# Late rows gathered by two transfers, early tiles added singly, 8 KB store runs, and batch 0's q as f32 at the head of SyncE's queue

## The chip, the cores and the metric

The kernel runs on one core of one Trainium2 chip. The metric is device microseconds of that core: the median of several executions, all fast unless said otherwise (one execution of the kernel before, 435.10 us, was slow and is left out). Profiles are single executions, and their span is some 2 us shorter than the timed execution.

TensorE (PE) does the matrix products, VectorE (DVE) and ScalarE (ACT) the elementwise work. SyncE (SP) and GpSimd (POOL) mostly issue transfers. The profile counts 16 DMA engines, and all transfers are shown on them.

## The reference

Linear attention with an ELU feature map is followed by a spectral mix, for 8 batches, 8 heads, 576 positions and head size 64 (so D = 512):

```python
q_p, k_p = phi(q), phi(k)                       # phi(x) = where(x > 0, x, exp(x) - 1) + 1
kv  = einsum('bhsd,bhse->bhde', k_p, v);  z = sum(k_p, axis=2)
x   = (q_p @ kv) / (q_p . z)                    # reordered to (B, S, D)
X   = rfft(x, axis=1)[:, :64]                   # 64 modes
Y   = X @ (w_r + i w_i), one complex 512x512 matrix for each mode
u   = x + irfft(Y);  out = u + relu(u @ w_ch)   # f32, 9.44 MB
```

The weights w_r and w_i are 64 matrices each of 512x512 f32, 134 MB in all. Reading them is the bulk of the work.

## The kernel before

The kernel has three stages. First, attention and forward transform, while q, k, v and the first weights arrive. Then the 64 modes, one pair of weight matrices after another, cast from f32 to bf16 by the transfer. Last, a tail after the final weights: the last 8 modes' contribution is added to every output tile, and the tiles are stored. A tile is 128 rows of 512 f32, 2 KB to a partition.

The loads of the start; all three inputs are cast to f16 by transfers that GpSimd issues:

```python
nc.sync.dma_start(out=id16, in_=id16_dr.ap())         # at the head of SyncE's queue
nc.sync.dma_start(out=fwd_sb, in_=fwd_dr.ap())
...
def load(b):
    for nm, src in (("q", q), ("k", k), ("v", v)):
        t = sA.tile([128, NHP, NJ * Dh], F16, tag=f"{nm}16", bufs=2, ...)
        pin(nc.gpsimd.dma_start(out=t, in_=src[b] ...))
```

In the tail, the last modes' rows (`last`: 128 partitions of mode, real/imaginary, batch; a y half and a z half, 2 KB together) are moved to where the later products want them. For each batch that is partitions 48 to 63 and again 112 to 127 of the tile `YZ[b]`:

```python
for b in (2, 3, 0, 1, 4, 5, 6, 7):
    for h in range(1 if b < N_LEAD else 2):           # 14 transfers of 32 KB
        nc.gpsimd.dma_start(out=YZ[b][64 * h + 48 : 64 * h + 64, :, :], in_=last[b::B, :, :])
```

The tiles of batches 0 and 1 use `last` directly. From the fifth pair of tiles on, the product reads `YZ`. Each pair is finished by a product, one VectorE add of 1024 columns and one store:

```python
def finish(n):                                        # cut
    add_inverse(n, 0)                                 # TensorE, reads last or YZ
    on_bank(n, {0, 1}, nc.vector.tensor_tensor(out=x, in0=acc, in1=x, op=ALU.add))
    store(t0, 2)                                      # SyncE: 512 KB in runs of 4 KB
...
store(0, 1); relu(0, 1); rectified(1); channels(2)
add_inverse(0, 0, (1,)); ...add of tile 1...; store(1, 1)
channels(3); rectified(2); finish(1)
rectified(3); finish(2)
```

## Time and profile before

| | |
|---|---|
| time, median of 3 (429.36 us of 6, later) | 429.39 us (428.43 to 429.47) |
| DMA share of the chain that ended last | 73% |
| last product with the final weights starts | 394.31 us |
| first store issued | 398.08 us |
| last add on VectorE ends | 420.14 us |
| span | 427.4 us |

The profile's page of the kernel before. The two rows cover the span in 40 equal slices: the mean busy share of the DMA engines in tenths, and what they moved in GB/s. The last line gives the chain of waits by engine.

```profile
DMA  8999999999999999999999999999999999996698
GB/s 146 207 208 209 209 210 209 211 214 214 218 212 214 213 214 213 215 212 214 213 213 214 213 214 212 214 214 214 214 213 214 214 214 212 213 213 135 211 404 313
DMA 73%; PE 12%; DVE 6%; issue 5%; POOL 1%; ACT 1%; DVEq 0%; POOLq 0%
```

DMA is busy nearly throughout. The slices from 385 to 395 us (135 GB/s, the last weights and the start of the tail) and from 395 to 406 us (211 GB/s) are the slack ones; the second is well short of the roughly 400 GB/s that stores reach afterwards. (The row counts the casting loads by the bytes they write. The page has 82.26 MB in their queue and 163.93 MB read from memory, so they read twice as much.)

### The profile page before, as it was taken

To read this page: it belongs to the slowest core of one execution; us is meant where nothing else is said; L and a number is where in the kernel's file an instruction comes from. 1 tells how busy PE (TensorE), PEld (TensorE's weight loads), DVE (VectorE), ACT (ScalarE), POOL (GpSimd) and SP (SyncE) were. 2 spreads that over 40 slices of the span, in tenths; PEclk is the share of its full clock that TensorE was granted. 3 is DMA by queue.
4 is the path that set the end of the run, shared out by engine and by line. 5 is a ranking of instruction groups with operands and counts; after the bars stand their busy time and mean duration, and the time that the engine had idled before them with its cause. 6 is when DMAs were issued, how large, how long until landed. Compare 5 with 4: busy or idle time off the path is not lost.

```text
span 427.4 us, 6617 instructions
## 1 busy us (share of the span) xinstructions
PE 285.4 (67%) x2692; PEld 158.9 (37%) x2692; DVE 212.1 (50%) x432; ACT 153.7 (36%) x240; POOL 95.6 (22%) x173
## 2 busy tenths in 40 slices
PE   0357777788119765655333697777788788999991
PEld 0346655564003433333111333433333344374320
DVE  0699998956003755556200433443354344421893
ACT  3588666640102100000000244444353353431781
POOL 4233223212201322112112122122122122010600
PEclk9996666656557755555555569999898899799996
DMA  8999999999999999999999999999999999996698
GB/s 146 207 208 209 209 210 209 211 214 214 218 212 214 213 214 213 215 212 214 213 213 214 213 214 212 214 214 214 214 213 214 214 214 212 213 213 135 211 404 313
DMA packets 35854, 92.46 MB, mean 216 GB/s; under 512 B 3216, under 2 KB 16400, under 8 KB 35824
## 3 DMA queue, kind: packets, MB, share of 16 engines
q0 software_dynamic: 32256, 82.26, 99.0%
q1 hardware_dynamic: 3568, 9.78, 6.0%
q8 instruction: 21, 0.34, 0.3%
q14 instruction: 9, 0.07, 0.0%
HBM read 163.93 MB, written 9.44 MB: 406 GB/s over the span
## 4 chain that ended last, share of the span: by engine, by line
DMA 73%; PE 12%; DVE 6%; issue 5%; POOL 1%; ACT 1%; DVEq 0%; POOLq 0%
DMA wr<-in_moe_w_r_dram 48%; DMA wi<-in_moe_w_i_dram 13%; DMA pick_sb<-row_pick 4%; DMA q<-in_q_dram 4%; DMA k<-in_k_dram 4%; PE P L349 3%; PE acc L616 3%; DVE x L267 2%; PE acc L655 2%; PE z L579 1%; PE zb L606 1%; PE eps L557 1%; PE zb L605 1%; DVE qe L195 1%; ACT ke L182 1%
## 5 line engine op out<-in xcount | busy, mean ns | idle before, releaser
L349 PE MATMUL P<-wi,xt_c 128*32 128x512 bf16 x252 | 37.8, 536 | 39.7 <-DMA wi<-in_moe_w_i_dram 39.7
L360 ACT CAST ys<-P 128x512 f16<-128x512 f32 x31 | 18.2, 586 | 125.3 <-PE P L349 125.3
L110 POOL DMA_DIRECT2D wr<-in_moe_w_r_dram x64 | 34.0, 532 | 124.4 <-PE P L349 102.2
L110 POOL DMA_DIRECT2D wi<-in_moe_w_i_dram x65 | 34.5, 531 | 117.7 <-PE P L349 82.8
L358 DVE CAST ys<-P 128x512 f16<-128x512 f32 x32 | 22.1, 691 | 72.3 <-PE P L349 72.2
L349 PEld LDWEIGHTS <-xt_c 128*32 128x32 bf16 x504 | 28.9, 155 | 76.3 <-issue 65.2
L349 PE MATMUL P<-wr,xt_c 128*32 128x512 bf16 x252 | 37.5, 532 | 23.0 <-DMA wr<-in_moe_w_r_dram 20.8
L538 DVE TENSOR_TENSOR x_main<-ya,x_main 128x512 f32<-128x512 f32 x32 | 22.1, 691 | 39.7 <-PE ya L534 39.6
L557 PE MATMUL eps<-wch,xTw 128*128 128x512 f16 x144 | 41.3, 415 | 0.0
L146 PEld LDWEIGHTS <-qT 64*128 64x128 f16 (+1 forms) x640 | 23.3, 126 | 41.1 <-issue 20.7
L365 PE MATMUL yt<-pick_sb,ys 128*128 128x16 f16 x252 | 16.5, 175 | 25.5 <-DMA pick_sb<-row_pick 15.1
L540 ACT CAST x16w<-x_main 128x512 f16<-128x512 f32 x32 | 19.8, 618 | 34.7 <-DVE x_main L538 34.7
L565 ACT CAST E<-eps 128x512 f16<-128x512 f32 (+1 forms) x40 | 21.3, 543 | 26.6 <-PE eps L557 26.6
L146 PE MATMUL num<-kv,qT 64*128 64x65 f16 (+1 forms) x320 | 13.5, 223 | 22.5 <-ACT kv L242 18.7
L365 PEld LDWEIGHTS <-ys 128*128 128x128 f16 x252 | 12.2, 102 | 40.5 <-issue 17.8
L182 ACT ACTIVATE qe<-q 128x1152 f16<-128x1152 f16 x16 | 17.7, 1155 | 22.7 <-DMA q<-in_q_dram 22.7
L211 PE MATMUL qTp<-id,qe 128*128 128x128 f16 x144 | 16.8, 312 | 12.4 <-DVE qe L195 12.0
L267 DVE TENSOR_TENSOR x<-num,rd 128x512 f16<-128x512 f32 x32 | 22.1, 692 | 1.1
L146 PE MATMUL nw<-kv,qT 64*128 64x65 f16 (+1 forms) x320 | 19.6, 236 | 1.1 <-DVE x_tail L508 0.9
L211 PEld LDWEIGHTS <-qe 128*128 128x128 f16 x144 | 14.7, 147 | 13.2 <-DVE qe L195 12.0
L182 ACT ACTIVATE ke<-k 128x1152 f16<-128x1152 f16 x16 | 17.7, 1155 | 4.9 <-DMA k<-in_k_dram 4.9
L665 ACT ACTIVATE acc<-acc 128x512 f32<-128x512 f32 x34 | 18.1, 581 | 2.3 <-PE acc L616 1.7
(101 smaller groups left out, 451.8 us busy)
## 6 DMA issues: line engine op xcount, KB each, us to landing
wr<-in_moe_w_r_dram POOLq DMA_DIRECT2D x64, 512.0 KB, 18.8
wi<-in_moe_w_i_dram POOLq DMA_DIRECT2D x63, 512.0 KB, 18.9
out_dram<-x_main SPq DMA_DIRECT2D x14, 512.0 KB, 5.8
q<-in_q_dram POOLq DMA_DIRECT2D x8, 576.0 KB, 13.1
k<-in_k_dram POOLq DMA_DIRECT2D x8, 576.0 KB, 14.5
v<-in_v_dram POOLq DMA_DIRECT2D x8, 576.0 KB, 16.7
out_dram<-x_main SPq DMA_DIRECT2D x4, 256.0 KB, 3.6
out_dram<-x_tail SPq DMA_DIRECT2D x2, 512.0 KB, 5.3
```

Of the source, the lines that this page charges most:

```text
L110: tc.keep_in_program_order(nc.gpsimd.dma_start(out=w[:, dcs], in_=rows_of[:, dcs, :]))
L146: mm = nc.tensor.matmul(num[hpo][orow, c0 : c0 + 65], qT[rows, hpp, h2, cols], kv_sb[rows, hpp, h2, :])
L182: pin(nc.scalar.activation(out=ev[:, c], in_=heads(nm, b)[:, c], func=AF.Exp))
L211: nc.tensor.transpose(qT_ps[:, j].rearrange("p t r -> p (t r)"), phi["q", b][:, hpp, j].rearrange("p o d -> p (o d)"), id16,)
L267: nc.vector.tensor_tensor(out=dst.rearrange("p (o c d) -> p o c d", o=2, c=4), in0=nv[:, :, :, 0:64], in1=rden.unsqueeze(3).broadcast_to([ ...
L349: nc.tensor.matmul(P[dc * 32 : dc * 32 + 32, :], xt_cols(dc, t, kk), w[:, dc, :], start=(t == 1), stop=(t == 0), tile_position=(0, dc * 32),)
L358: fixed(nc.vector.tensor_copy(out=st, in_=P))
L365: nc.tensor.matmul(yt_ps[:, ec, kk % 8, :], st[:, ec * 128 : ec * 128 + 128], pick_sb)
L538: pin(nc.vector.tensor_tensor(out=x, in0=acc, in1=x, op=ALU.add))
L540: pin(nc.scalar.copy(out=x16w[t], in_=x))
L557: nc.tensor.matmul(e_ps, xT[:, c, :], wch16[:, c, :], start=(c == 0), stop=(c == NDC - 1))
L565: pin(nc.scalar.copy(out=dst, in_=e_ps[:, cols]))
```

## The change

The change has five parts. Batch 0's q is loaded without a cast (f32) from the head of SyncE's queue, so that bytes move before GpSimd's first cast load. The 14 small gathers become two, one on SyncE and one on GpSimd. Tiles 2 and 3 are added and stored singly, so that stores start sooner. Batches 4 to 6 are stored as four tiles at once, in runs of 8 KB. The transposed last rows are copied in halves by two engines. The diff, cut to its core:

```diff
-    nc.sync.dma_start(out=id16, in_=id16_dr.ap())
-    nc.sync.dma_start(out=fwd_sb, in_=fwd_dr.ap())
...
+            if (nm, b) == ("q", 0):
+                for c in range(2):
+                    t = sA.tile([128, 2, NJ * Dh], F32, tag="x16", bufs=2, name=f"q32_{c}")
+                    pin(nc.sync.dma_start(out=t, in_=rows_in[:, c::2, :]))
+                    raw[nm, b, c] = t
+                pin(nc.sync.dma_start(out=id16, in_=id16_dr.ap()))
+                pin(nc.sync.dma_start(out=fwd_sb, in_=fwd_dr.ap()))
+                continue
...
-    YZ = [sW.tile([128, 2, D], F16, tag="YZ", bufs=B, name=f"YZ{b}") for b in range(B)]
+    YZ_all = sW.tile([128, B, 2, D], F16, tag="YZ", bufs=1, name="YZ_all")
+    YZ = [YZ_all[:, b] for b in range(B)]
...
+    QUADS = (4, 5, 6)
...
+        if t0 < B * NJJ and t0 // NJJ in QUADS:
+            if t0 % NJJ:
+                store(t0 - 2, NJJ)
+            return
...
-    pin(nc.scalar.copy(out=last[:, 0, :], in_=y_ps.rearrange("p c r -> p (c r)")))
+    pin(nc.scalar.copy(out=last[:, 0, COLS[0]], in_=y_ps[0].rearrange("p c r -> p (c r)")))
+    pin(nc.vector.tensor_copy(out=last[:, 0, COLS[1]], in_=y_ps[1].rearrange("p c r -> p (c r)")))
...
-    for b in (2, 3, 0, 1, 4, 5, 6, 7):
-        for h in range(1 if b < N_LEAD else 2):
-            nc.gpsimd.dma_start(out=YZ[b][64 * h + 48 : 64 * h + 64, :, :], in_=last[b::B, :, :])
+    for h, eng in enumerate((nc.sync, nc.gpsimd)):
+        eng.dma_start(
+            out=YZ_all[64 * h + 48 : 64 * h + 64].rearrange("r b z d -> r b (z d)"),
+            in_=last.rearrange("p z d -> p (z d)"),
+        )
...
-    channels(3)
     rectified(2)
-    finish(1)
+    for i in range(2):
+        add_inverse(1, 0, (i,))
+        add_one(1, i)
+    channels(3)
     rectified(3)
```

## The prediction

> **What bounds it now.** The page's DMA row is at 9 tenths in nearly every slice, the software queue takes 99% of 16 engines' span, and the chain of waits is 73% DMA, nearly all weight loads. The other engines have slack until the last weights land (394.3 us, timeline). Then a 33 us tail writes 9.44 MB. There the packet records show about 403 GB/s from 406 us to 425.5 us, while the last add on VectorE ends at 420.1 us: the stores are DMA-bound too, with some 4 us of backlog at the end. Only from 399 to 406 us does DMA run short: 145 to 370 GB/s, a loss of about 1.9 us of full-rate transfer.
>
> **The change, piece by piece.**
>
> 1. *Batch 0's q as f32 on SyncE's queue.* Before, the first cast load issues at 1.26 us and moves bytes from about 3.5 us; the identity and DFT loads at SyncE's head issue at 0.74 us and move from 1.9 us, only 0.19 MB. After, 1.18 MB of q moves from about 2.0 us at some 390 GB/s (estimate), and one 2.85 us cast load leaves GpSimd's queue. About 1.5 us of empty DMA is filled; the 0.19 MB comes later, costing about 0.7 us (73 ns a packet of 1280 B, 17 ns one of 256 B, 16 engines). Net 0.6 to 0.8 us; it reaches the end, as the stream has no gap up to 390 us.
>
> 2. *Late rows by two transfers.* 14 issues of 0.48 us on GpSimd (397.2 to 403.9 us) become two, one on SyncE. TensorE does not wait for them now, so the gain is indirect: 0.5 MB moves before the first store, where DMA is empty (394.3 to 398.5 us), not between stores. The Trainium skill ("DMA: Bandwidth & Descriptors", "Issuing engines are not separate DMA queues") says all queues share the 16 engines; the trace agrees: the stores' rate falls to 235 GB/s where row packets interleave.
>
> 3. *First four tiles singly.* Tiles 2 and 3 are stored about 1.2 and 0.6 us sooner, filling the hole at 401 us. Two more stores of 2 KB runs cost 0.1 us (87 ns per 2 KB, 163 per 4 KB). Items 2 and 3 together: 1.2 to 1.8 us.
>
> 4. *8 KB runs, batches 4 to 6.* At best 3 to 4% on 3.1 MB (estimate), 0.25 us. Holding the first pair back 1.14 us should just be covered by the backlog.
>
> 5. *Transposed last rows copied by halves, copies moved.* The zl products keep TensorE busy until 396.0 us, so y0 starts no earlier: 0 to 0.1 us.
>
> **Sum.** 0.7 + 1.5 + 0.2 = 2.4 us, all on the DMA path. Predicted 427.0 us, 8 in 10 between 425.4 and 428.6. Faster by over 2%: 1%; within 2%: 98%; slower: 1%.
>
> **What would show it.** Right: last weights land 0.5 to 1 us earlier; the first transfer carries q at about 2 us; two row transfers land before about 400.5 us; the DMA rate stays above 350 GB/s from 400 us; the first store stays about 3.8 us after the last weights land; tail 1.5 to 2 us shorter; 8 KB packets take under 326 ns. Wrong: the weights end unmoved (item 1), a DMA hole at 409 to 412 us (item 4), TensorE waiting for YZ (item 2).
>
> **What would make it wrong.** A gather that writes 16 partitions at a low rate and blocks stores; SyncE issuing the gather so slowly that the first store slips; the slow DMA engine, which ends 4 us after the others, not profiting from item 1.

## More of the kernel before

The tail of the kernel before, in stretches of 2 us. Columns: the stretch, then busy us of PE, PEld, DVE, ACT and POOL with instruction counts, TensorE's granted clock, DMA share, GB/s. (The share adds up the times of all packets, so it can exceed 1 where packets of one engine overlap.)

```profile
396.00:398.00 2.00, 1.70 (x9) 0.71 (x8) 1.66 (x3) 0.80 (x3) 0.77 (x2) 1.00 0.00 0
398.00:400.00 2.00, 2.00 (x11) 0.99 (x10) 0.99 (x3) 1.82 (x4) 2.00 (x5) 1.00 0.56 189
400.00:402.00 2.00, 2.00 (x10) 0.75 (x9) 2.00 (x2) 1.75 (x5) 2.00 (x5) 1.00 0.69 238
402.00:404.00 2.00, 2.00 (x12) 0.41 (x10) 2.00 (x3) 1.72 (x5) 1.92 (x5) 1.00 0.96 341
404.00:406.00 2.00, 2.00 (x16) 0.68 (x14) 1.97 (x3) 1.73 (x4) 0.00 (x0) 1.00 0.96 341
406.00:408.00 2.00, 2.00 (x14) 0.60 (x14) 1.94 (x2) 1.71 (x4) 0.00 (x0) 1.00 1.03 412
```

Two different shortages stand here. Until 402 us the engines are partly idle (0.56, 0.69). From 402 to 406 us they are busy (0.96) and yet move only 341 GB/s.

The transfers issued from 396 to 405 us in the kernel before; the last figure is the median of us from issue to landing:

```profile
out_dram<-x_main SPq DMA_DIRECT2D x2, 256.0 KB, 2.6
YZ<-last POOLq DMA_DIRECT2D x14, 32.0 KB, 2.8
```

## The result, and the profile after

The changed kernel takes 429.2 us (428.75 to 430.86, 6 runs), the kernel before 429.36 us in the same rounds. The ratio is 1.0003, with a 95% interval of 0.9983 to 1.0023. Ratios here and below are the mean time of one kernel's fast runs over that of the other's of the same rounds, so they are not quite the ratio of the medians. Where a ratio is turned into microseconds, it is its distance from 1 times 429.4 us. A gain of 2.4 us was forecast and none came. A second job read the same (after_again, 1.0004).

The tail of the changed kernel, in the same stretches and columns:

```profile
396.00:398.00 2.00, 1.95 (x9) 0.99 (x9) 1.45 (x3) 1.27 (x3) 0.56 (x1) 1.00 0.31 61
398.00:400.00 2.00, 2.00 (x10) 0.95 (x9) 1.72 (x3) 1.87 (x5) 0.00 (x0) 1.00 1.16 172
400.00:402.00 2.00, 0.82 (x4) 0.22 (x2) 1.22 (x1) 0.89 (x2) 0.00 (x0) 1.00 0.92 153
402.00:404.00 2.00, 1.47 (x7) 0.49 (x8) 0.51 (x1) 0.75 (x2) 0.00 (x0) 1.00 1.06 393
404.00:406.00 2.00, 2.00 (x13) 0.56 (x10) 2.00 (x3) 1.72 (x4) 0.00 (x0) 1.00 0.89 362
406.00:408.00 2.00, 2.00 (x17) 0.58 (x15) 1.97 (x2) 1.61 (x4) 0.00 (x0) 1.00 1.00 401
```

From 398 to 402 us the DMA share is about 1, so the engines are fully occupied, and they move only 172 and 153 GB/s. From 400 us TensorE runs dry (0.82 us of 2), and from 402 us VectorE (0.51 us of 2). The waits of VectorE and TensorE from 396 us on in the changed kernel say for what; the figures are us in total, times, longest:

```profile
DVE x_main L708 <- PE acc L627: 2.6, 2, 2.2
PE acc L627 <- DMA YZ_all<-last: 1.7, 2, 1.0
```

The kernel before had no wait of TensorE on `YZ` in its tail, and VectorE's adds there waited 0.6 us at most:

```profile
DVE x_main L695 <- PE acc L616: 0.6, 1, 0.6
```

The transfers issued from 395 to 400 us in the changed kernel, with the us from issue to landing:

```profile
out_dram<-x_main SPq DMA_DIRECT2D x4, 256.0 KB, 5.2
YZ_all<-last SPq DMA_DIRECT2D x1, 256.0 KB, 5.1
YZ_all<-last POOLq DMA_DIRECT2D x1, 256.0 KB, 6.2
```

A store of one tile takes 5.2 us where it took 2.6. Tile 0's store is issued at 397.37 us, and the packet records show no packet of any store before 400.48 us. The gathers' packets run from 397.3 to 401.2 us: 524 KB in 3.8 us, 137 GB/s (128 to 145 GB/s in the four profiles that have two whole gathers). GpSimd's 4 KB packets take 599 ns at the median, and 16 engines at 4096 B in 599 ns are 109 GB/s. (That is this profile; in after_again, the same kernel, the median is 498 ns.)

The gain at the start is there. The kernel before, then the changed kernel, from 0 to 6 us, same columns:

```profile
0.00:2.00 2.00, 0.00 (x0) 0.00 (x0) 0.63 (x3) 1.27 (x1) 0.94 (x5) 1.00 0.07 16
2.00:4.00 2.00, 0.00 (x0) 0.00 (x0) 0.00 (x0) 0.22 (x2) 2.00 (x4) 1.00 0.72 121
4.00:6.00 2.00, 0.00 (x0) 0.00 (x0) 0.00 (x0) 0.00 (x0) 1.89 (x3) 1.00 1.16 172
```

```profile
0.00:2.00 2.00, 0.00 (x0) 0.00 (x0) 0.63 (x3) 1.27 (x1) 0.95 (x5) 1.00 0.15 13
2.00:4.00 2.00, 0.00 (x0) 0.00 (x0) 0.00 (x0) 0.22 (x2) 2.00 (x4) 1.00 0.85 275
4.00:6.00 2.00, 0.00 (x0) 0.00 (x0) 0.18 (x1) 1.16 (x1) 1.87 (x3) 1.00 1.08 354
```

The plain f32 load moves 275 GB/s where the old queue heads moved 121. (The f32 bytes count in full, the cast ones by half.) The first store is issued at 397.37 us instead of 398.08 us.

### The profile page after: what moved, and what is told of

Its sections match the earlier page's. It is cut to its first block, busy times and chain, and to the rows that moved or that the text cites. A ratio compares the mean times of both kernels' runs of the same rounds, so it can differ in the third digit from the quotient of the medians.

```text
span 427.8 us, 6610 instructions
## 1 busy us (share of the span) xinstructions
PE 281.6 (66%) x2692; PEld 158.3 (37%) x2692; DVE 214.5 (50%) x434; ACT 154.1 (36%) x241; POOL 88.1 (21%) x159
## 4 chain that ended last, share of the span: by engine, by line
DMA 67%; PE 15%; DVE 7%; issue 7%; ACT 1%; POOL 1%; DVEq 0%; POOLq 0%; ACTq 0%
DMA wi<-in_moe_w_i_dram 43%; DMA wr<-in_moe_w_r_dram 14%; DMA k<-in_k_dram 9%; PE P L359 3%; PE acc L627 2%; DVE x L277 2%; PE z L590 2%; PE acc L666 2%; DMA YZ_all<-last 1%; ACT ke L190 1%; PE zl L345 1%; PE yp L603 1%; PE zb L617 1%; PE zb L616 1%; PE eps L568 1%
## 5 line engine op out<-in xcount | busy, mean ns | idle before, releaser
L359 PE MATMUL P<-wi,xt_c 128*32 128x512 bf16 x252 | 36.2, 517 | 42.2 <-DMA wi<-in_moe_w_i_dram 42.1
L568 PE MATMUL eps<-wch,xTw 128*128 128x512 f16 x144 | 40.3, 407 | 0.0
L190 ACT ACTIVATE qe<-q 128x1152 f16<-128x1152 f16 (+1 forms) x16 | 17.8, 1156 | 18.0 <-DMA q<-in_q_dram 17.9
```

The lines of the kernel that those rows point to most:

```text
L190: pin(nc.scalar.activation(out=ev[:, c], in_=heads(nm, b, c), func=AF.Exp))
L359: nc.tensor.matmul(P[dc * 32 : dc * 32 + 32, :], xt_cols(dc, t, kk), w[:, dc, :], start=(t == 1), stop=(t == 0), tile_position=(0, dc * 32),)
L568: nc.tensor.matmul(e_ps, xT[:, c, :], wch16[:, c, :], start=(c == 0), stop=(c == NDC - 1))
```

## The experiments

**Theory 1 (ports).** A gather of 262 KB into 16 neighbouring partitions moves at about a quarter of the full rate, because those partitions share few SBUF ports. The Trainium skill ("SBUF — State Buffer", "Door 1: The DMA port swizzle") says that groups of four partitions share a port, that partitions 0 to 15 reach 4 of 16 ports and about 109 GB/s at best, 32 neighbours 8 ports, and all 128 all 16. By its table, partitions 48 to 63 lie on ports 8, 10, 12 and 14. If that holds here, the two gathers occupy all DMA engines for nearly 4 us, keep the first stores back and starve TensorE of `YZ`.

**Theory 2 (quads).** The loss comes from holding back half of batches 4 to 6, so that DMA runs short at 413 us. The changed kernel's DMA share from 412 to 416 us was 0.93 against 1.03 before. The kernel before, then the changed kernel, same columns:

```profile
412.00:416.00 4.00, 4.00 (x26) 1.15 (x26) 3.97 (x4) 3.51 (x7) 0.00 (x0) 1.00 1.03 406
412.00:416.00 4.00, 4.00 (x22) 0.89 (x22) 4.00 (x4) 3.63 (x8) 0.00 (x0) 1.00 0.93 370
```

**Theory 3 (SyncE's queue).** The gather stands ahead of the stores in SyncE's queue and keeps them back by its place, not by its rate.

**Theory 4.** The early load gains nothing at the end, because the slowest DMA engine does not profit.

### The gather undone, the gather alone

a_gather14 is the changed kernel with the old 14 gathers:

```diff
-    for h, eng in enumerate((nc.sync, nc.gpsimd)):
-        eng.dma_start(out=YZ_all[64 * h + 48 : 64 * h + 64].rearrange(...), in_=last.rearrange(...))
+    for b in (2, 3, 0, 1, 4, 5, 6, 7):
+        for h in range(1 if b < N_LEAD else 2):
+            nc.gpsimd.dma_start(out=YZ[b][64 * h + 48 : 64 * h + 64, :, :], in_=last[b::B, :, :])
```

> The changed kernel with the late rows gathered by the old 14 small transfers; all else kept. Ports theory (two gathers of 262 KB, each written into 16 neighbouring partitions, move at about 108 GB/s, hold every DMA engine from 397.6 to 401.4 us, keep the first stores back and starve TensorE, VectorE idle 2.2 us): the first stores move by 398.5 us, VectorE has no wait over 1 us in the tail, time 426 to 427.5 us. Quad theory (the loss comes from holding back half of batches 4 to 6): the hole at 413 us stays and the time stays at 428.5 us or more.

b_gather2 is the kernel before with the opposite edit alone.

> The kernel before with the two gathers alone. Ports theory: slower by 1.5 to 3 us (431 to 432.5 us), with TensorE waiting on YZ for 1 to 2 us and the stores of tiles 0 and 1 not moving before about 400.5 us. Quad theory: within 0.5 us of before.

a_gather14 read 428.19 us, ratio to before 0.9966 (0.9945 to 0.9988). b_gather2 read 430.73 us, ratio 1.0023 (1.0000 to 1.0047), about 1.0 us slower (1.25 by the medians; the interval just reaches none). Both moved in the direction of theory 1, both by less than it expected: a_gather14's median lies above the stated 426 to 427.5 us, and b_gather2's below the stated 431 to 432.5 us. In the traces, a_gather14's first store packet moves at 397.65 us, as expected; b_gather2's moves at 399.58 us, earlier than the expected 400.5.

The tail of a_gather14, same columns:

```profile
396.00:398.00 2.00, 2.00 (x11) 0.89 (x10) 1.48 (x3) 1.83 (x4) 2.00 (x5) 1.00 0.28 96
398.00:400.00 2.00, 2.00 (x11) 0.86 (x9) 1.66 (x3) 1.78 (x4) 2.00 (x5) 1.00 0.84 272
400.00:402.00 2.00, 2.00 (x12) 0.61 (x10) 1.90 (x3) 1.49 (x3) 2.00 (x6) 1.00 0.94 318
402.00:404.00 2.00, 2.00 (x16) 0.68 (x14) 2.00 (x3) 1.73 (x4) 0.46 (x1) 1.00 0.96 344
```

TensorE and VectorE no longer run dry. From 398 to 402 us the engines move 272 and 318 GB/s instead of 172 and 153, at shares of 0.84 and 0.94 instead of 1.16 and 0.92. VectorE waits 0.8 us for the add of tile 0, as in the changed kernel, and at most 0.4 us for any later add. The store of one tile lands in 2.9 us again:

```profile
out_dram<-x_main SPq DMA_DIRECT2D x4, 256.0 KB, 2.9
```

a_gather14 also makes `YZ` eight tiles again. That is not the cause: probe_end below keeps `YZ_all` as one tile beside the 14 gathers, and TensorE has no wait on it in its tail.

The kernel before with the two gathers shows the new waits, here of VectorE and of TensorE:

```profile
DVE x_main L696 <- PE acc L617: 3.9, 4, 2.5
PE acc L617 <- DMA YZ_all<-last: 1.7, 1, 1.7
```

VectorE waits 3.9 us and the time grows by only about 1.0 us. This is consistent with the backlog of stores at the end of the kernel before: VectorE's last add ends at 420.1 us, the span at 427.4 us. VectorE has slack to lose, and the time depends on what the DMA engines carry. (A lowered granted clock may be part of the 3.9 us: TensorE had 0.50 from 404 to 406 us in this profile.)

To read the cost on one chip, the changed kernel and a_gather14 were run once more together.

> The changed kernel once more, on one chip with the next two, so that the cost of the gathers is read from the same rounds. If the gathers cost what the traces suggest (first store to last packet 28.5 us against 26.9 us): 1.2 to 1.7 us slower than a_gather14_again and equal to before within 0.8 us.

> a_gather14 once more: 0.9945 to 0.9985 of before. If it is no faster than after_again here, the gather is not the cause and the earlier difference lay between the chips.

(The spans of 28.5 and 26.9 us in the first of these are not found again in the traces: from the issue of the first store to the end of the last packet they give 29.2 and 27.9 us.)

after_again read 429.52 us, ratio 1.0004 (0.9987 to 1.0021). a_gather14_again read 427.87 us, ratio 0.9961 (0.9949 to 0.9973). The two gathers cost 1.65 us by the medians and 1.84 us by the means, at or just above the upper end of the expected 1.2 to 1.7. The two large gathers also carry 65 KB more than the 14, which skip the second half for batches 0 and 1; how much of the cost that is was not tested. The cost is as much as all the other parts of the change gain together.

### Is it the place in the queue?

a_gather2_pool is the changed kernel with both gathers on GpSimd:

```diff
-    for h, eng in enumerate((nc.sync, nc.gpsimd)):
+    for h, eng in enumerate((nc.gpsimd, nc.gpsimd)):
```

> The changed kernel with both gathers issued by GpSimd, so that SyncE's queue holds stores alone. Ports theory: no better than the changed kernel, 429 to 430.5 us, with the same wait of TensorE for YZ. Rival, that the gather ahead of the stores on SyncE's queue keeps them back: 428 to 428.4 us, as a_gather14.

It read 430.98 us, ratio 1.0048 (1.0023 to 1.0073), slower than both expectations. Freeing SyncE's queue does not help, so theory 3 falls. The packet records show how: tile 0's store is issued at 399.02 us and its packets start at 400.41 us, sooner after the issue than in the changed kernel (1.4 against 3.1 us), but the first 128 store packets then take 3.1 us instead of 1.6. Held back or slowed, 262 KB are out 4.5 to 4.7 us after the issue, against 1.7 us in a_gather14. Why it is slower still than the changed kernel is not settled. Its profiled run also shows TensorE's granted clock at 0.72 from 396 to 400 us, where the changed kernel had 1.00, so its tail began late for a reason of its own.

### The disputed rate by itself

probe_end is a_gather14 (with `YZ_all` as one tile) and six transfers after the last store, each waiting for the one before, all with the same 128 source runs of 2 KB:

```diff
+    x_end = x_of(pairs[-1][1])
+    nc.vector.memset(x_end, 0.0)                      # waits for the last store
+    for z in range(2):
+        nc.vector.tensor_copy(out=last[:, z, :], in_=x_end)
+    for eng in (nc.sync, nc.gpsimd):
+        for rows_to in (slice(48, 64), slice(0, 128), slice(0, 128, 8)):
...                                               # dst: YZ_all[rows_to], or YZ_all[:, 0] for all 128
+            eng.dma_start(out=dst, in_=flat_last)
```

> a_gather14 with six transfers appended after the last store, one after another, each of the same 128 runs of 2 KB of the late rows: into partitions 48 to 63, into all 128, into every eighth; first from SyncE, then from GpSimd. It is for its trace, not its time. Ports theory: 16 neighbouring partitions reach 4 of 16 ports, so 262 KB take about 2.4 us of moving (near 108 GB/s) from either queue; every eighth partition reaches 8 ports and takes about 1.2 us; 128 partitions about 0.65 us. Rival, that 16 destination rows with one row to each DMA engine are slow in themselves: every eighth partition is as slow as the neighbours. Rival, that the queue is the cause: the SyncE three are fast and the GpSimd three slow, whatever the partitions.

Its output is correct and its time, 451.3 us, means nothing. The transfers of probe_end in order of issue, by windows that hold one each: SyncE to 16 neighbours, to 128, to every eighth; then GpSimd likewise. The last figure is us from issue to landing.

```profile
YZ_all<-last SPq DMA_DIRECT2D x1, 256.0 KB, 4.2
...
YZ_all<-last SPq DMA_DIRECT2D x1, 256.0 KB, 2.3
...
YZ_all<-last SPq DMA_DIRECT2D x1, 256.0 KB, 3.0
...
YZ_all<-last POOLq DMA_DIRECT2D x1, 256.0 KB, 4.0
...
YZ_all<-last POOLq DMA_DIRECT2D x1, 256.0 KB, 2.3
...
YZ_all<-last POOLq DMA_DIRECT2D x1, 256.0 KB, 2.9
```

The queue makes next to no difference; the destination makes nearly all of it. By the table of the skill's page ("SBUF — State Buffer") the neighbours lie on 4 ports, every eighth partition on 8 and all 128 on 16. At its asymptotes of 109, 218 and 436 GB/s, 262 KB would take 2.4, 1.2 and 0.6 us (an estimate from that page). The neighbours should then land 1.8 us and every eighth 0.6 us after the 128. Measured are 1.9 and 1.7 us, and 0.7 and 0.6 us. Every eighth partition is 16 destination rows too, and yet it is faster, so the rival of 16 rows being slow in themselves falls. Theory 1 stands, and here with nothing else moving.

One lesson of reading: for SyncE's gather to neighbours the packet records span only 1.62 us (162 GB/s) against 0.83 us for the 128, while the landing differs by 1.9 us. The packets' own durations understated what the slow destination cost.

### The 8 KB runs

a_gather14_noquad and y_early_noquad (y_early is the last experiment below) store batches 4 to 6 in pairs again:

```diff
-    QUADS = (4, 5, 6)
+    QUADS = ()
```

> As a_gather14, and batches 4 to 6 stored in pairs again (4 KB runs). Ports theory with quads as predicted: slower than a_gather14 by 0.1 to 0.4 us. Quad theory: faster than a_gather14 by 0.5 us or more.

> y_early with batches 4 to 6 stored in pairs again. If 8 KB runs are worth the 0.25 us of the prediction: 0.1 to 0.4 us slower than y_early was against before (0.9961), so 0.9963 to 0.9970. If what they gain in rate is lost in the hole that holding back opens: no difference beyond the noise.

a_gather14_noquad read 428.13 us, ratio 0.9967, beside a_gather14's 0.9966 in the same job: no difference. y_early_noquad read 428.22 us, ratio 0.9966 (0.9953 to 0.9980), beside 0.9961 and 0.9945 for y_early in other jobs. A gain of 0.25 us is within the intervals, none is too. Theory 2 falls as the main cause: the quads lose nothing once the gather is undone. What they lose beside the gathers was not run. The hole at 412 to 416 us (370 against 406 GB/s) is worth about 0.35 us, an estimate from these two rates, and may be part of why the gathers cost more in the changed kernel than in the kernel before. In a_gather14 the 8 KB packets take about 316 ns, 415 GB/s over 16 engines, and the 4 KB ones of its tail about 163 ns, 402 GB/s.

### The early load, and the single adds

b_q32 is the kernel before with the changes to the loads and to the features of batch 0, nothing else. b_singles is the kernel before with the new order and the single adds of tiles 2 and 3:

```diff
-    channels(3)
     rectified(2)
-    finish(1)
+    for i in range(2):
+        add_inverse(1, 0, (i,))
+        add_one(1, i)
+    channels(3)
```

> The kernel before with batch 0's q as f32 on SyncE's queue alone. As predicted: the last weights land 0.5 to 1 us earlier and the time is 0.5 to 0.9 us shorter, 428.5 to 428.9 us. Rival (the slowest DMA engine does not profit): last weights at 394.2 us or later, time unmoved.

> The early load alone, beside the others: 0.5 to 0.9 us faster than before, as predicted (first reading 0.9985).

> The kernel before with tiles 2 and 3 added and stored singly alone. The prediction's sizing (a hole of 1.9 us of full-rate transfer, most of it filled): 1.0 us or more faster. What the traces now suggest (only about 0.5 us of it was idle engines, the rest slow packets): 0.3 to 0.6 us faster, 428.8 to 429.2 us.

> The single adds alone, beside the others: 0.3 to 0.6 us faster than before (first reading 0.9989); with the prediction's sizing 1.0 us or more.

> The yardstick of this job, the same kernel as a_gather14: 0.9955 to 0.9975 of before, as in its two earlier readings.

| part | ratio, first job | ratio, second job | gain in us, by the ratios | by the medians |
|---|---|---|---|---|
| b_q32 | 0.9985 (0.9961 to 1.0009) | 0.9979 (0.9942 to 1.0016) | 0.6, 0.9 | 0.6, 0.7 |
| b_singles | 0.9989 (0.9969 to 1.0009) | 0.9982 (0.9948 to 1.0016) | 0.5, 0.8 | 0.2, 0.5 |
| a_gather14, three jobs | 0.9966, 0.9961 | 0.9958 (0.9924 to 0.9992) | 1.5, 1.7, 1.8 | 1.3, 1.6, 1.2 |

In the second job all three shared one chip. There one execution of the kernel before took 434.04 us, and it raises every gain that is read from that job's ratios by some 0.4 us. So the medians are the better reading: the parts, 0.7 and 0.5 us, add up to what a_gather14 gained with both, 1.2 us. Each part's interval includes no gain at all, so the sizes are rough, but two readings of each agree in sign. The cast on VectorE that follows the last weights' product starts from 394.45 to 394.81 us in the four profiles without the early load, 394.63 us on average. In the thirteen with it, it starts from 393.19 to 394.04 us, 393.58 us on average, but for a_gather2_pool's 394.48 us (left out of the average, as its profile has a lowered clock). So the last weights are done about 1 us earlier, and theory 4 falls in what it says of the slowest engine. Not all of that 1 us is seen in the time of b_q32; where the rest went, if it is not noise, is open.

### A version that beats both: the y half moved into the empty stretch

The large gather is slow, but that need not cost anything where no store waits. Nothing moves from 394 to 396 us in the kernel before or in the changed one. The y half of the late rows is ready there, about 1 us before the z half (copies end at 395.04 and 396.00 us in the changed kernel). y_early is the changed kernel with this edit:

```diff
     pin(nc.vector.tensor_copy(out=last[:, 0, COLS[1]], ...))
+    for h, eng in enumerate((nc.sync, nc.gpsimd)):
+        eng.dma_start(out=YZ_all[64 * h + 48 : 64 * h + 64, :, 0, :], in_=last[:, 0, :])
...
...                                               # the two gathers of both halves go
+    for b in (2, 3, 0, 1, 4, 5, 6, 7):
+        for h in range(1 if b < N_LEAD else 2):
+            nc.gpsimd.dma_start(out=YZ[b][64 * h + 48 : 64 * h + 64, 1, :], in_=last[b::B, 1, :])
```

> The changed kernel with its two gathers carrying the y half alone (131 KB each), issued as soon as y is copied, about 1.5 us earlier, into the stretch in which DMA is empty, and the z half by 14 transfers of 16 KB on GpSimd. If the gather's cost is engine time taken from the stores, the y half becomes nearly free: 0.4 to 0.8 us faster than a_gather14, 427.4 to 427.8 us. If the large gathers still overrun the first stores: no faster than a_gather14.

> y_early beside a_gather14 on one chip. If the y half costs nothing when it moves in the empty stretch: 0.4 to 0.8 us faster than a_gather14_third. If the first stores are held up by it after all, or the idle engine time only moves: within 0.3 us of it.

y_early read 427.33 us, ratio 0.9961 (0.9942 to 0.9979). y_early_again read 427.44 us, ratio 0.9945 (0.9912 to 0.9978), beside a_gather14_third's 428.22 us and 0.9958 on the same chip. That is 0.6 us faster by the means and 0.8 us by the medians, as expected; in its first job, set against a_gather14 of another job, it showed only part of that. One reading does not fit: y_early_noquad was 0.35 us slower by the medians than a_gather14_again in the same job (428.22 against 427.87 us), though the quads had shown no difference in a_gather14. So the size of the gain rests on one job. The tail of y_early, same columns:

```profile
396.00:398.00 2.00, 2.00 (x11) 0.87 (x10) 1.56 (x3) 2.00 (x5) 2.00 (x5) 1.00 0.80 185
398.00:400.00 2.00, 2.00 (x11) 0.82 (x10) 1.66 (x3) 1.55 (x3) 2.00 (x5) 1.00 0.92 305
```

DMA is busy at 0.80 from 396 to 398 us, where it was at 0.28 in a_gather14, and afterwards more is left for the stores: 305 GB/s against 272. y_early gives correct results and has the lowest medians, 1.6 and 2.0 us below the kernel before in its two jobs.

## Why the prediction was wrong

- **Item 2, the two gathers, is the step that failed.** The prediction said that "0.5 MB moves before the first store, where DMA is empty". At the 403 GB/s of the stores 524 KB would take 1.3 us (an estimate). The packets moved from 397.3 to 401.2 us, at 137 GB/s, under and ahead of the stores, and the second gather landed only at 402.5 us. It cost 1.65 to 1.84 us (after_again against a_gather14_again) instead of a gain. The prediction counted bytes at full rate and instructions saved. It named "a gather that writes 16 partitions at a low rate and blocks stores" among the risks and gave it no term in the sum, though the size was at hand: the 109 GB/s that the skill's page gives for four ports make 2.4 us of each gather (an estimate from that page).
- **"TensorE does not wait for them now"** was right of the kernel before and did not carry over: TensorE waited 1.7 us in the changed kernel, a wait that the prediction had named as a sign of failure. The 14 small transfers delivered batches 2 and 3 first; a large one delivers everything at its end.
- **Item 3, the single adds, was right in kind and sized too high.** With item 2 it was to bring 1.2 to 1.8 us; alone it brought 0.2 to 0.5 us by the medians (0.5 to 0.8 by the ratios). The forecast took the whole shortfall of 1.9 us as idle DMA. The stretches of the profile before show the engines idle only until 402 us; from 402 to 406 us they were busy at 0.96 and moved 341 GB/s. The likely reason is the row packets in between: there a row packet of 2 KB took 115 ns on average and a store packet of 4 KB 175 ns, against 85 and 162 ns from 406 to 410 us. Earlier stores could not fill busy engines.
- **Item 1, the early load, held:** 0.6 and 0.7 us by the medians (0.6 and 0.9 by the ratios) against a stated 0.6 to 0.8 us, within an interval that includes none.
- **Item 4, the 8 KB runs,** was stated at 0.25 us. The runs cannot tell that from nothing. A hole, which was named as a sign of failure for 409 to 412 us, came a little later (DMA share 0.93 from 412 to 416 us). The likely reason is that VectorE's stall had removed the backlog that was to cover it: without the stall, a_gather14 has 1.03 there.
- **Item 5 fits,** as far as single profiles tell: from the cast after the last weights to the first store it takes 3.44 us before (394.64 to 398.08) and 3.33 us after (394.04 to 397.37).

With the gather undone, what is left gains 1.2 to 1.6 us by the medians (1.5 to 1.8 by the ratios). The forecast's tail gain also counted on the gather lying in the empty stretch; y_early put half of it there and came to 1.6 and 2.0 us. The forecast 2.4 us appears only in one ratio (0.9945), which the execution of 434.04 us raises. So item 2 turned the gain into none, and the smaller size of item 3 is likely the rest of the miss.

## What to carry to other kernels

Before merging small transfers, ask where they land: a large transfer into few neighbouring partitions can hold all DMA engines at a fraction of their rate (here 137 of some 400 GB/s), and stores on its own queue and on another were out late alike (4.7 and 4.5 us after their issue instead of 1.7). Small transfers into the same partitions, spaced by their issue, were the better form on a busy stretch here, and the large one belongs where nothing else moves. When reading a low DMA rate, look at the busy share beside it: idle engines can be given work earlier, busy slow ones cannot.

## What the Trainium skill lacked or had wrong

- "DMA: Bandwidth & Descriptors", "Rules for kernel authors", advises to coalesce many small transfers into one large one, since under 64 KB they are mostly overhead. Here 14 transfers of 32 KB beat two of 256 KB by 1.65 us, all of them into runs of 16 partitions. The rule lacks an exception for a large transfer into few partitions beside other traffic. "SBUF — State Buffer" does have the port limit, and the runs agree with it: landing 1.9 and 1.7 us later on 4 ports than on 16, 0.7 and 0.6 us later on 8.
- "SBUF — State Buffer", "Can I just issue two DMAs to hit both halves?", says that two transfers to the two partition halves serialize. The changed kernel agrees: 524 KB took 3.8 us, 137 GB/s, though its halves lie on different ports; one such half alone moved at 162 GB/s in probe_end. That stalled writes hold up an engine's other queues is said only of transfers between cores ("DMA: Bandwidth & Descriptors", "Back-pressure in remote DMA"). Something like it shows here within one core: a 256 KB store took 5.2 us to land instead of 2.6 us, and stores on a queue of their own landed in 4.8 us (a_gather2_pool).
- No page that we read says that packet durations in a trace can understate a port-limited write: 1.62 us of packets against 0.83 us, while the landings differed by 1.9 us.
